# Weight blocks requested from a buffer that was read a step earlier, and a new order at the end of the second transform step

## The chip, the cores and the metric

The kernel runs on one core of one Trainium2 chip. The metric is the device time of one execution in microseconds (us). The engines are TensorE (PE; its weight loads are PEld), VectorE (DVE), ScalarE (ACT), GpSimd (POOL) and SyncE (SP). Each runs its own instructions in the order of the program and waits on semaphores for the others. SyncE and ScalarE also issue transfers (SPq, ACTq); an instruction that issues one waits, like any other, until what it needs is free, and what stands behind it on its engine waits too.

## The reference

```python
h_mlp  = np.maximum(pos_emb @ w1, 0.0) @ w2           # (S, 64) -> (S, 128), S = 12480
h_filt = h_mlp * np.exp(-0.01 * np.arange(S))[:, None]
y = irfft(rfft(x * v, 2 * S) * rfft(h_filt, 2 * S), 2 * S)[:S]   # along the sequence
x = x * y                                             # (S, 128)
h = x @ moe_w_in                                      # (S, 2048)
x = (h * np.clip(h + 3.0, 0.0, 6.0) / 6.0) @ moe_w_out
h = x @ moe2_w_in
out = np.where(h > 0, h, np.exp(np.minimum(h, 0.0)) - 1.0) @ moe2_w_out
```

The result is float32. The four weight matrices of the two feed-forward layers come as float64.

## The kernel before, in words

The long convolution is done as a transform in steps, all of them matmuls with tables.

**First step.** Products `x * v` and the hidden filter layer go through a table of cosines and sines of length 98 into `Au` (two halves of 64 channels each: half 0 lies in `qb`, half 1 in `au`) and `Rk`.

**Second step.** The 91 frequencies are taken in twelve `OCTETS` of eight (the last, number 11, has three). For an octet `o`: `second_r` (L370) transforms the filter's hidden part in place with a table `gm`, ScalarE copies it back (L371); `second_h` (L379) multiplies by `w2`, ScalarE copies the result into a buffer `hss[o % 2]` (L382, two copies) and adds a negated third part (L383); `second_u(o, hf)` (L389) transforms the signal of half `hf` with `gm` into a PSUM bank; `second(o, hf, z)` is the complex product: two VectorE multiplications (L403) into one of two pairs of buffers, then one GpSimd addition (L408) that writes `Au` back. Written h9, r10, z(9,0) and so on below. `gm` comes in groups of four frequencies, eight of them in SBUF; `load_gm0` (L248) on SyncE requests a group two octets ahead. PSUM has four buffers of two banks, tags `px` and `py` with two each. Octets 0 to 9 go one after the other, both halves of each. For octets 10 and 11, half 0 of both comes first, then half 1 of both, with each product cut into pieces of four frequencies.

**Third step.** `third` (L416) takes four channels at a time: eight matmuls into a bank pair `q`, a ScalarE copy of one part into `tb` (L420), and two VectorE operations (L422) that write `Q` over `qb`. 16 groups for half 0, 18 for half 1 (the last three have two, one and one channel). Behind every eight channels of half 1 a piece of `xT` (728 KB) is requested on SyncE into the part of `au` that was read.

**Fourth step.** `fourth` (L496) makes the output in 33 calls, tables `ti` streaming through five buffers on SyncE (L464), VectorE multiplying by `x` (L541).

**Feed-forward layers.** From 286 us to the end, TensorE alternates L616 and L660; this part is not touched.

**Weight conversion.** Beside all this the float64 weights are turned into float32, in 32 blocks of 128 x 256 (`weight_steps`, a generator). One turn k is: VectorE L208, L209, L210 on block k, a GpSimd addition (L213), `load(k + 3)` (L186) into one of three raw buffers, `begin(k + 1)` (ScalarE L196 and L197), `store(k - 1)` (L191, on ScalarE's queue). `convert(rate)` adds `rate` to a counter and takes a turn whenever it passes one: in each `second` call, each `third` group (not the last four) and each call of the fourth step, with `RATE[0]`, `RATE[1]`, `RATE[2]`. The requests go out on SyncE in the second step and on ScalarE afterwards. What is left is done at the fourth step's end.

Of the kernel before, what the change touches and what calls it, by code (L numbers as in the profile page):

```python
# [18 lines left out]
S, D, FO, FF = 12480, 128, 64, 2048  # L19
# [11 lines left out]
HD = D // 2  # L31
# [65 lines left out]
def tile_kernel(ctx, tc, xc, vc, xT, posT, w1_d, w2_d, moe_w, t1_d, gm_d, cs_d, ti_d, rows_d, column_d, ratio_d, outT):  # L97
# [11 lines left out]
    def bank(name, shape, tag=None):  # L109
        if tag is None:  # L110
            turn[0] += 1
            tag = "px" if turn[0] % 2 else "py"
        return ps.tile(shape, F32, tag=tag, name=name)
# [21 lines left out]
    qb = big.tile([128, 2 * QW], F32, name="qb")  # L135
# [19 lines left out]
    OCT = 8  # L155
# [24 lines left out]
    def weight_steps(jobs, raws, es, rs):  # L180
        v = nc.vector

        def load(k):
            if k < len(jobs):
                i, c = jobs[k]
                queue[0].dma_start(raws[k % 3].bitcast(I64), moe_w[i][:, c:c + WC])  # L186

        def store(k):
            if k >= 0:
                i, c = jobs[k]  # L190
                nc.scalar.dma_start(w_dram[i][:, c:c + WC], rs[k % 4])  # L191

        def begin(k):
            if k < len(jobs):
                w = raws[k % 3].rearrange("p (n t) -> p n t", t=2)
                nc.scalar.activation(es[k % 2], w[:, :, 1], AF.Abs)  # L196
                nc.scalar.mul(rs[k % 4].bitcast(I32), w[:, :, 0].bitcast(U32), 2.0 ** -29)  # L197

        for k in range(3):
            load(k)  # L200
        yield
        begin(0)
        yield
        for k in range(len(jobs)):
            w = raws[k % 3].rearrange("p (n t) -> p n t", t=2)
            e = es[k % 2]
            i, r = (z.bitcast(I32) for z in (e, rs[k % 4]))
            v.scalar_tensor_tensor(e, e, LEAST, most.to_broadcast([128, WC]), op0=ALU.max, op1=ALU.min)  # L208
            v.tensor_scalar(i, i, 3, 0x3FFFFFFF, op0=ALU.logical_shift_left, op1=ALU.bitwise_and)  # L209
            v.scalar_tensor_tensor(  # L210
                i, w[:, :, 1].bitcast(I32), -0x40000000, i, op0=ALU.bitwise_and, op1=ALU.bitwise_or
            )
            nc.gpsimd.tensor_tensor(out=r, in0=i, in1=r, op=ALU.add)  # L213
            load(k + 3)
            begin(k + 1)
            store(k - 1)
            yield
        store(len(jobs) - 1)

    def cut(buf, size, n):  # L220
        return [buf[:, i * size:(i + 1) * size] for i in range(n)]

    weights = weight_steps(JOBS, cut(cv, 2 * WC, 3), cut(cv[:, 6 * WC:], WC, 2), cut(cv[:, 8 * WC:], WC, 4))
    RATE = (0.67, 0.28, 0.42)
    due = [0.0]

    def convert(n):
        due[0] += n
        while due[0] >= 1:
            due[0] -= 1  # L230
            next(weights, None)
# [13 lines left out]
    def load_gm0(n):  # L245
        if n < len(KGROUPS):
            k0, nk = KGROUPS[n]
            nc.sync.dma_start(gms[n % len(gms)][:, :nk], gm_d[:, k0:k0 + nk])  # L248
# [5 lines left out]
    def groups(sizes):  # L254
        return list(zip(np.cumsum([0] + sizes[:-1]).tolist(), sizes))

    KGROUPS = groups([KC] * (NK // KC) + [NK % KC])
    OCTETS = groups([OCT] * (NK // OCT) + [NK % OCT])
# [80 lines left out]
    for kind, n in order:  # L339
# [13 lines left out]
    bctx = ctx.enter_context(ExitStack())  # L353
    bp = bctx.enter_context(tc.tile_pool(name="bp", bufs=1)).tile([128, HW + 2 * MW], F32, name="bp")
    hss = [z.rearrange("p (k r d) -> p k r d", r=3, d=D) for z in (rest[:, HB:HB + HW], bp[:, :HW])]
    mms = [
        [z.rearrange("p (d k r) -> p d k r", r=2, k=OCT) for z in zs]
        for zs in (
            (rest[:, MB:MB + MW], rest[:, RF + D:RF + D + MW]), (bp[:, HW:HW + MW], bp[:, HW + MW:]),
        )  # L360
    ]

    def gm_of(k):
        return gms[k // KC % GN][:, k % KC]

    def second_r(o):
        k0, nk = OCTETS[o]
        r = bank("r", [128, OCT, N2], "px")
        for j in range(nk):
            nc.tensor.matmul(r[:, j], lhsT=Rk[:, k0 + j], rhs=gm_of(k0 + j), start=True, stop=True)  # L370
        nc.scalar.copy(Rk[:, k0:k0 + nk], r[:, :nk])  # L371

    def second_h(o):
        k0, nk = OCTETS[o]
        hr = [bank("h", [128, OCT, D], "px") for r in range(2)]
        for j in range(nk):
            for r in range(2):
                p = slice(r * FO, (r + 1) * FO)
                nc.tensor.matmul(hr[r][:, j], lhsT=Rk[p, k0 + j], rhs=w2s[p], start=True, stop=True)  # L379
        hs = hss[o % 2]  # L380
        for r in range(2):
            nc.scalar.copy(hs[:, :nk, r], hr[r][:, :nk])  # L382
        nc.scalar.mul(hs[:, :nk, 2], hs[:, :nk, 1], -1.0)  # L383

    def second_u(o, hf, tag="py"):
        k0, nk = OCTETS[o]
        z = bank("z", [128, OCT, D], tag)
        for j in range(nk):
            nc.tensor.matmul(z[:, j], lhsT=gm_of(k0 + j), rhs=Au[hf][:, :, k0 + j], start=True, stop=True)  # L389
        return z  # L390
# [3 lines left out]
    def second(o, hf, z, size=OCT, rate=0):  # L394
        k0, nk = OCTETS[o]
        for a in range(0, nk, size):
            n = min(size, nk - a)
            m1, m2 = (m[products[0] % 2][:, :, :n] for m in mms)
            products[0] += 1
            h = hss[o % 2][:, a:a + n, :, hf * HD:(hf + 1) * HD]  # L400
            flat = h[:, :, 0].unsqueeze(3).to_broadcast([128, n, HD, 2])
            for mm, h in ((m1, flat), (m2, h[:, :, 1:].rearrange("p k r d -> p k d r"))):
                nc.vector.tensor_tensor(  # L403
                    out=mm.rearrange("p d k r -> p k d r"),
                    in0=z[:, a:a + n].rearrange("p k (d r) -> p k d r", r=2), in1=h, op=ALU.mult,
                )
            convert(rate)
            nc.gpsimd.tensor_tensor(  # L408
                out=Au[hf][:, :, k0 + a:k0 + a + n], in0=m1, in1=m2[:, :, :, ::-1], op=ALU.add
            )  # L410

    def third(hf, s0, nd):
        q = bank("q", [128, 2, 4, N2])
        for j in range(nd):
            for r in range(2):
                nc.tensor.matmul(  # L416
                    q[:NK, r, j], lhsT=Au[hf][:, s0 + j, :, r], rhs=cs[:, r * N2:(r + 1) * N2], start=True, stop=True
                )
        qs = tile_of(stb, "tb", [NK, 4, N2], 3)
        nc.scalar.copy(qs[:, :nd], q[:NK, 1, :nd])  # L420
        for o, op in enumerate((ALU.add, ALU.subtract)):
            nc.vector.tensor_tensor(  # L422
                out=Q[:NK, hf, o * HN:(o + 1) * HN, s0:s0 + nd].rearrange("p g d t -> p d g t"),
                in0=q[:NK, 0, :nd].rearrange("p d (g t) -> p d g t", t=2),
                in1=qs[:, :nd].rearrange("p d (g t) -> p d g t", t=2), op=op,
            )

    last = len(OCTETS) - 1
    second_r(0)
    second_r(1)  # L430
    for o in range(last - 1):
        if o == 0:
            z = second_u(o, 0)
            second_h(o)
        else:
            second_h(o)
            z = second_u(o, 0)
        second(o, 0, z, rate=RATE[0])
        if o:
            second_r(o + 1)  # L440
        if o == last - 2:
            second_r(last)
        second(o, 1, second_u(o, 1), rate=RATE[0])
        for n in range(2 * (o > 0)):
            load_gm0(2 * (o - 1) + GN + n)
    zs = {}
    for o in (last - 1, last):
        second_h(o)
        zs[o] = second_u(o, 0)
    for hf in range(2):  # L450
        for o in (last - 1, last):
            second(o, hf, second_u(o, 1, "px") if hf else zs[o], OCT // 2)
    bctx.close()
    stb = sctx.enter_context(tc.tile_pool(name="stb", bufs=3, side="right"))
    lds = cctx.enter_context(tc.tile_pool(name="ldi", bufs=1, reuse_waits="tile"))
# [4 lines left out]
    def load_ti(m0):  # L460
        if m0 < NM:
            n = min(2, NM - m0)
            ti = tile_of(lds, "ti", [NK, 2, 2, H1], TB)
            nc.sync.dma_start(ti[:, :n].rearrange("p j r a -> p j (r a)"), ti_d[:, m0:m0 + n])  # L464
            tis[m0] = ti
# [6 lines left out]
    a, b = xload.pop()  # L472
    nc.sync.dma_start(xp[:, a:b], xT[:, a:b])
    for s0, nd in groups([4] * 16):
        third(0, s0, nd)
        convert(RATE[1])
    for s0, nd in groups([4] * 15 + [2, 1, 1]):
        third(1, s0, nd)
        if (s0 + nd) % EX == 0:
            a, b = xload.pop(0)  # L480
            nc.sync.dma_start(xp[:, a:b], xT[:, a:b])
        if s0 and s0 % 12 == 0 and s0 // 12 < TB:
            load_ti(s0 // 6)
        convert(RATE[1] if s0 < 56 else 0)

# [44 lines left out]
    for m0 in range(0, NM, 2):  # L530
# [9 lines left out]
        o = START.get((m0, 1), 0)  # L540
# [5 lines left out]
        if m0 == 14:  # L546
            nc.vector.tensor_tensor(out=x0[:, 1], in0=xp[:, :TT], in1=x0[:, 0].bitcast(F32), op=ALU.subtract)
        convert(RATE[2])
    convert(1000)
# [189 lines left out]
```

## Time and profile before

| | |
|---|---|
| median of 3 runs | 1362.53 us (1362.12 to 1362.95) |
| the profiled execution | 1363.29 us, of which the span is 1361.5 us |
| busy share of the span | PE 99%, PEld 84%, DVE 84%, ACT 73%, POOL 29% |
| granted TensorE clock, mean | 0.998 of full speed |
| second step ends, third begins (first L416) | 172.99 us |
| fourth step begins (first L496) | 239.05 us |
| feed-forward layers begin (first L616) | 285.80 us |

Times in the rows are microseconds from the start of the span. A releaser is inferred from semaphore events; a wait for several is put down to the one that came last. A busy TensorE is not one at its peak, since matmuls are pipelined, so idle time is the safer reading.

### The profile page before, as it was taken

How to read it: one execution, taken by the hardware profiler on the slowest of the kernel's cores; microseconds unless marked ns; L12 is line 12 of the kernel's file. 1: busy time of each engine (PE TensorE's matmuls, PEld its weight loads, DVE VectorE, ACT ScalarE, POOL GpSimd, SP SyncE). 2: the span in 40 equal slices, each digit the busy share in tenths (PEclk: the TensorE clock that was granted, in tenths of full speed). 3: DMA queues.
4: the chain of work that ended last, by engine and by line, in shares of the span. 5: the costliest groups of instructions: out<-in, count | busy, mean ns of one | idle time of the engine just before them, and what ended most of it. 6: DMA issues, size and time to landing. Idle time of an engine off the chain costs nothing.

```text
span 1361.5 us, 20839 instructions
## 1 busy us (share of the span) xinstructions
PE 1341.5 (99%) x8154; PEld 1149.4 (84%) x8154; DVE 1145.8 (84%) x1230; ACT 991.5 (73%) x1171; POOL 396.2 (29%) x280
## 2 busy tenths in 40 slices
PE   9999988999999999999999999999999999999998
PEld 9999887987888888888888888888888888888898
DVE  6748677689988888888888888888888888888897
ACT  5666523268888778877888778877888778877876
POOL 1027620124322233222322232222322232222223
PEclk9999999999999999999999999999999999999999
DMA  8924316650000000000000000000000000000000
GB/s 271 258 66 133 92 53 229 205 191 1 1 8 9 8 8 1 9 8 8 1 8 8 9 9 1 8 8 8 1 8 8 8 8 1 9 8 8 8 4 16
DMA packets 32491, 58.15 MB, mean 43 GB/s; under 512 B 3880, under 2 KB 12169, under 8 KB 32393
## 3 DMA queue, kind: packets, MB, share of 16 engines
q1 hardware_dynamic: 25048, 47.85, 11.3%
q10 hardware_dynamic: 7344, 8.98, 2.1%
q8 instruction: 64, 1.05, 0.3%
q14 instruction: 35, 0.28, 0.1%
HBM read 46.23 MB, written 10.58 MB: 42 GB/s over the span
## 4 chain that ended last, share of the span: by engine, by line
PE 76%; DVE 4%; issue 2%; ACT 1%; DMA 0%; POOL 0%; ACTq 0%; DVEq 0%; POOLq 0%
PE h L616 37%; PE o L660 37%; PE y L496 3%; DVE gs L650 2%; DVE qb L422 1%; DVE g L637 1%; DMA ti<-in_ti 0%; POOL a L629 0%; ACT tb L420 0%; DVE g L639 0%; ACT a L628 0%; ACT gs L645 0%; DVE cv L208 0%; ACT cv L196 0%; DVE cv L210 0%
## 5 line engine op out<-in xcount | busy, mean ns | idle before, releaser
L660 PE MATMUL o<-gs,w 128*128 128x512 f32 (+1 forms) x2400 | 567.1, 384 | 0.5 <-DVE gs L650 0.4
L660 PEld LDWEIGHTS o<-gs,w 128*128 128x128 f32 x2400 | 445.3, 188 | 88.6 <-DVE gs L650 0.9
L629 POOL TENSOR_SCALAR a<-a 128x1024 f32<-128x1024 f32 (+1 forms) x200 | 296.3, 1481 | 718.3 <-ACT a L628 718.3
L650 DVE TENSOR_TENSOR gs<-g,gs 128x1024 fp32r<-128x1024 f32 (+1 forms) x400 | 483.1, 1208 | 4.5 <-ACT gs L645 3.7
L645 ACT CAST gs<-g 128x1024 fp32r<-128x1024 f32 (+1 forms) x400 | 410.3, 1026 | 54.7 <-DVE g L637 53.1
L637 DVE SCALAR_TENSOR_TENSOR g<-a,h 128x1024 f32<-128x1024 f32 (+1 forms) x200 | 238.7, 1194 | 120.5 <-ACT a L626 120.2
L616 PE MATMUL h<-xs,w 128*128 128x512 f32 (+1 forms) x1200 | 302.0, 387 | 0.6 <-DVE g L637 0.4
L616 PE MATMUL h<-x,w 128*128 128x512 f32 (+1 forms) x1200 | 299.0, 385 | 0.3 <-ACT a L628 0.3
L628 ACT ACTIVATE a<-h 128x1024 f32<-128x1024 f32 (+1 forms) x200 | 201.3, 1007 | 91.6 <-PE h L616 90.5
L616 PEld LDWEIGHTS h<-xs,w 128*128 128x128 f32 x1200 | 223.6, 188 | 48.8 <-DVE g L637 1.6
L616 PEld LDWEIGHTS h<-x,w 128*128 128x128 f32 x1200 | 223.1, 188 | 43.8 <-issue 0.5
L626 ACT ACTIVATE a<-h,bounds 128x1024 f32<-128x1024 f32 (+1 forms) x200 | 219.2, 1096 | 52.1 <-PE h L616 51.7
L639 DVE SCALAR_TENSOR_TENSOR g<-a,h 128x1024 f32<-128x1024 f32 (+1 forms) x200 | 237.5, 1187 | 0.2 <-POOL a L629 0.2
L196 ACT ACTIVATE cv<-cv 128x256 f32<-128x256 f32 x32 | 14.1, 441 | 67.2 <-DVE cv L210 27.0
L213 POOL TENSOR_TENSOR cv<-cv 128x256 int32<-128x256 int32 x32 | 23.4, 730 | 111.1 <-DVE cv L210 111.1
L422 DVE TENSOR_TENSOR qb<-q,tb 91x512 f32<-91x512 f32 (+2 forms) x68 | 39.3, 648 | 16.4 <-ACT tb L420 16.4
L408 POOL TENSOR_TENSOR qb<-qb,bp 128x1024 f32<-128x1024 f32 (+2 forms) x13 | 27.4, 2110 | 71.0 <-DMA qb<-in_gm 70.5
L496 PE MATMUL y<-ti,qb 91*64 91x98 f32 (+1 forms) x1024 | 45.9, 247 | 1.2 <-DMA ti<-in_ti 0.7
L496 PEld LDWEIGHTS y<-ti,qb 91*64 91x64 f32 x1024 | 45.4, 138 | 1.7 <-issue 1.2
L322 PE MATMUL pa<-t,cv 98*64 98x182 f32 x512 | 44.7, 318 | 0.0
L322 PEld LDWEIGHTS pa<-t,cv 98*64 98x64 f32 x512 | 37.7, 137 | 4.0
L416 PE MATMUL q<-cs,au 128*91 128x128 f32 x256 | 29.4, 274 | 5.8 <-DVE qb L422 5.8
(65 smaller groups left out, 803.5 us busy)
## 6 DMA issues: line engine op xcount, KB each, us to landing
uv<-in_xc SPq DMA_DIRECT2D x32, 196.0 KB
out_T<-y SPq DMA_DIRECT2D x23, 256.0 KB
au<-in_xT SPq DMA_DIRECT2D x8, 728.0 KB
qb<-in_gm SPq DMA_DIRECT2D x22, 256.0 KB
cv<-in_mw ACTq DMA_DIRECT2D x18, 256.0 KB
ti<-in_ti SPq DMA_DIRECT2D x32, 139.3 KB
uv<-in_vc SPq DMA_DIRECT2D x22, 196.0 KB
w_scratch<-cv ACTq DMA_DIRECT2D x32, 128.0 KB
```

The source lines that it names most:

```text
L322: nc.tensor.matmul(pa[f * HN:(f + 1) * HN, j, :2 * NK], lhsT=src(j, f), rhs=table[:, f], start=True, stop=True)
L422: nc.vector.tensor_tensor(out=Q[:NK, hf, o * HN:(o + 1) * HN, s0:s0 + nd].rearrange("p g d t -> p d g t"), in0=q[:NK, 0, :nd].rearrange("p ...
L496: nc.tensor.matmul(y[h * HD:(h + 1) * HD, off:off + w], lhsT=Q[:NK, h, j // 2, :, j % 2], rhs=ti[:, m - m0, r, H1 - w:], start=r == 0, sto ...
L616: nc.tensor.matmul(h[:, j], lhsT=wslice(2 * m - 2, a, 2 * u + j), rhs=x[:, b], start=i == 0, stop=i == 2)
L626: nc.scalar.activation(a, h, AF.Relu, bias=three)
L628: nc.scalar.activation(a, h, AF.Exp)
L629: nc.gpsimd.tensor_scalar(a, a, 1.0, 0.0, op0=ALU.min, op1=ALU.max)
L637: nc.vector.scalar_tensor_tensor(g, a, 6.0, h, op0=ALU.min, op1=ALU.mult)
L639: nc.vector.scalar_tensor_tensor(g, a, -1.0, h, op0=ALU.add, op1=ALU.max)
L645: nc.scalar.copy(t[:, 0], g)
L650: nc.vector.tensor_tensor(out=t[:, 1], in0=g, in1=t[:, 0].bitcast(F32), op=ALU.subtract)
L660: nc.tensor.matmul(o[:, :WID[t]], lhsT=wslice(2 * m - 1, a, 2 * u + j), rhs=gs[:, b, j], start=u == 0 and j == 0 and i == 0, stop=u == NU ...
```

## The change

The first two weight blocks, instead of three, are requested at the start, and turn k requests block k + 2, whose raw buffer was read in turn k - 1. The rates become 0.78, 0.3 and 0.45. The third step takes no turn in its first eight groups. In the second step octets 0 to 8 go as before; then come octets 9, 10, 11 with half 0 of all three (products in pieces of four, and for octet 9 a rate of 0.5 a piece), with r10 and r11 behind octet 9's product, and then half 1 of all three with whole products. Octet 11 gets a filter buffer of its own, `Rs`, over the part of `qb` that octets 0 and 1 used.

```diff
-        for k in range(3):
+        for k in range(2):
             load(k)
...
-            load(k + 3)
+            load(k + 2)
             begin(k + 1)
             store(k - 1)
...
-    RATE = (0.67, 0.28, 0.42)
+    RATE = (0.78, 0.3, 0.45)
...
+    Rs = qb[:, :3 * D * OCTETS[-1][1]].rearrange("p (k r d) -> p k r d", r=3, d=D)
...
+    last = len(OCTETS) - 1
+
+    def hs_of(o):
+        return Rs if o == last else hss[o % 2]
...
-        hs = hss[o % 2]
+        hs = hs_of(o)
...
-            h = hss[o % 2][:, a:a + n, :, hf * HD:(hf + 1) * HD]
+            h = hs_of(o)[:, a:a + n, :, hf * HD:(hf + 1) * HD]
...
-    for o in range(last - 1):
+    for o in range(last - 2):
...
-        if o == last - 2:
-            second_r(last)
         second(o, 1, second_u(o, 1), rate=RATE[0])
         for n in range(2 * (o > 0)):
             load_gm0(2 * (o - 1) + GN + n)
-    zs = {}
-    for o in (last - 1, last):
+    ends = range(last - 2, last + 1)
+    for o in ends:
         second_h(o)
-        zs[o] = second_u(o, 0)
-    for hf in range(2):
-        for o in (last - 1, last):
-            second(o, hf, second_u(o, 1, "px") if hf else zs[o], OCT // 2)
+        second(o, 0, second_u(o, 0), OCT // 2, rate=0.5 if o == last - 2 else 0)
+        if o == last - 2:
+            second_r(o + 1)
+            second_r(last)
+    for o in ends:
+        second(o, 1, second_u(o, 1, "py" if o == last - 1 else "px"))
...
-        convert(RATE[1])
+        convert(RATE[1] if s0 >= HD // 2 else 0)
```

## Rows read from the trace of the kernel before

**Rows 1.** Chain that ended last, in order of time: start us, us, what.

```profile
199.31 3.94 issue
...
257.20 6.14 DMA ti<-in_ti
```

**Rows 2.** Windows: stretch, its length, busy us of PE, PEld, DVE, ACT, POOL, PEclk, DMA share, GB/s.

```profile
172.99:239.05 66.06, 58.06 (x512) 56.19 (x513) 48.88 (x92) 22.37 (x49) 9.36 (x11) 1.00 0.45 145
203.35:239.05 35.70, 29.39 (x258) 28.08 (x257) 26.28 (x49) 13.54 (x30) 3.61 (x5) 1.00 0.66 218
239.05:285.62 46.57, 45.88 (x1024) 45.37 (x1024) 32.81 (x78) 11.85 (x29) 11.62 (x15) 1.00 0.71 213
```

**Rows 3.** Waits in the third step: us in total, times, longest us.

```profile
PE q L416 <- DVE qb L422: 7.5, 8, 1.7
```

**Rows 4.** Timeline of one conversion, third step: start, us, engine, line, idle before it.

```profile
187.66 0.41 DVE L208 SCALAR_TENSOR_TENSOR cv<-cv,bounds 128x256 f32<-128x256 f32 x1
...
188.43 0.43 DVE L210 SCALAR_TENSOR_TENSOR cv<-cv 128x256 int32<-128x256 int32 x1
188.94 0.34 ACTq L186 DMA_DIRECT2D cv<-in_mw  x1
...
189.38 0.43 ACT L196 ACTIVATE cv<-cv 128x256 f32<-128x256 f32 x1 [4.39 <-DVE cv L210]
...
190.05 1.53 ACT L420 COPY tb<-q 91x512 f32<-91x512 f32 x3
190.65 4.87 DVE L422 TENSOR_TENSOR qb<-q,tb 91x512 f32<-91x512 f32 x8 [1.79 <-ACT tb L420]
...
192.08 7.20 PE L416 MATMUL q<-cs,qb 128*91 128x128 f32 x64 [1.13 <-DVE qb L422]
```

**Rows 5.** Timeline from octet 8 to the third step's start.

```profile
142.06 2.06 PE L379 MATMUL h<-qb 64*128 64x128 f32 x32
...
149.36 0.43 DVE L210 SCALAR_TENSOR_TENSOR cv<-cv 128x256 int32<-128x256 int32 x1
149.69 2.06 PE L379 MATMUL h<-qb 64*128 64x128 f32 x32
149.87 1.23 DVE L403 TENSOR_TENSOR qb<-z,qb 128x1024 f32<-128x1024 f32 x1
...
153.65 0.42 DVE L210 SCALAR_TENSOR_TENSOR cv<-cv 128x256 int32<-128x256 int32 x1
...
154.57 0.38 SPq L248 DMA_DIRECT2D qb<-in_gm  x1
...
157.22 2.37 POOL L408 TENSOR_TENSOR qb<-qb,bp 128x1024 f32<-128x1024 f32 x1
...
158.03 0.93 PE L370 MATMUL r<-qb 128*128 128x128 f32 x6 [2.48 <-DMA qb<-in_gm]
...
159.00 0.48 ACT L371 COPY qb<-r 128x384 f32<-128x384 f32 x1 [2.39 <-PE r L370]
...
164.37 1.93 ACT L382 COPY qb<-h 128x1024 f32<-128x1024 f32 x2 [4.24 <-PE h L379]
...
166.33 1.06 ACT L383 ACTIVATE qb<-qb 128x1024 f32<-128x1024 f32 x1
...
169.13 1.28 POOL L408 TENSOR_TENSOR qb<-qb,bp 128x512 f32<-128x512 f32 x1
169.21 0.69 DVE L403 TENSOR_TENSOR qb<-z,qb 128x512 f32<-128x512 f32 x1 [1.09 <-POOL au L408]
...
172.99 13.26 PE L416 MATMUL q<-cs,qb 128*91 128x128 f32 x117 [2.31 <-POOL qb L408]
...
176.96 1.06 ACT L420 COPY tb<-q 91x512 f32<-91x512 f32 x2 [8.27 <-POOL au L408]
```

**Rows 6.** Windows: the granted clock (PEclk) behind the hole, columns as in rows 2.

```profile
160.00:162.00 2.00, 2.00 (x12) 2.00 (x10) 0.00 (x0) 0.13 (x1) 0.00 (x0) 0.50 0.19 61
```

**Rows 7.** Line L208 in 98 to 173: count, ns min/median/max, first and last start.

```profile
L208 DVE SCALAR_TENSOR_TENSOR cv<-cv,bounds x11: 411/435/1128, 102.8 to 164.8; 128x256 f32<-128x256 f32 x11
```

More of the change, by code (lines that the diff above doesn't have):

```diff
@@ L426, in third @@
             )
-    last = len(OCTETS) - 1
     second_r(0)
     second_r(1)
-    for o in range(last - 1):
+    for o in range(last - 2):
         if o == 0:
```

## The prediction

> **What bounds the kernel now.** I read the chain of waits first. Its traced part begins in the third step, and there the longest piece is no work: ScalarE waits 3.94 us before it may issue a weight load [rows 1]. The windows by stage say what that is worth: in 172.99 to 239.05 TensorE is busy for 58.06 of 66.06 us, so 8.0 us are lost, 6.3 of them in the second half; the fourth step is full (45.88 of 46.57) [rows 2]. The list of waits puts 7.5 of the 8.0 on VectorE's `L422` [rows 3]. The timeline of one conversion tells why [rows 4]: `load(k+3)` writes the raw buffer that `L210` of the same step still reads, so ScalarE, in order, stands until `L210` ends (188.43+0.43), issues the load at 188.94, does its two conversion operations, and only then copies the three groups that TensorE has meanwhile finished. VectorE, idle for 1.79, starts at 190.65, and TensorE, with no free bank, resumes at 192.08.
>
> The second step is TensorE's (7.63 us from one octet's `L379` to the next, 142.06 to 149.69, so 3.81 a call of `second`), until its end. There `L370` waits 2.48 us for the last `gm` group: SyncE could issue that load only at 154.57, behind a weight load that waited for the `L210` at 153.65; it landed 3.5 us later [rows 5]. After this hole the granted clock is 0.50, the 1.2 GHz level, in 160 to 162 [rows 6]. The third step begins at 172.99 when GpSimd has finished the first channels' sums, and its first copy waits until 176.96 for GpSimd's last sum of all [rows 5].
>
> **The weight request.** `load(k+2)` goes into the buffer that step k-1 read, free for a whole step. ScalarE then passes it at once. With a conversion every 1/0.30 = 3.33 groups, and 58.06/32 = 1.81 us of TensorE a group, the period is 6.05 us. ScalarE needs in it 3.33 x 0.51 + 0.34 + 2 x 0.43 and a store, some 3.2; VectorE 3.33 x 1.22 + 1.2 = 5.3 [rows 4]. Both are under 6.05, four banks lie between, so TensorE sets the pace. Of the 8.0 us about 0.5 at the hand-over to the fourth step stays: I take 7.4 off. Bounds: 8.0, and half of it, 3.7, if VectorE's 1.2 us block still empties the banks.
>
> The added wait: `begin(k+1)` needs a block that is now requested one step before it instead of two. Behind it on ScalarE stand the copies of `q`, and VectorE waits for those. The trace shows no landing of such a block by itself; the nearest rows are 3.5 us for 192 KB [rows 5] and 6.14 us for a `ti` pair in the fourth step [rows 1]. Three groups give 5.4 us. So a conversion costs between nothing and 0.7, over the four in the second half 0 to 2.8; I take 0, since half a microsecond of ScalarE is covered by the banks. In the second step the requests are SyncE's and only let `gm` loads pass earlier.
>
> **The rates.** The counts: 18 x 0.78 + 2 x 0.5 = 15 turns before the third step (13 now), 22 x 0.30 = 6.6 in it (8 of 30 x 0.28 now), so 13 conversions are left for the fourth step as now. Two conversions move under the second step's TensorE. VectorE's cost there is not the third step's: `L208` takes 0.41 to 1.13 us [rows 7], and two conversions in successive calls end 4.28 us apart (149.36, 153.65) against 3.81 of TensorE [rows 5]. At 0.78 there are runs of three and four such calls (2-4, 6-9, 11-13, 15-18); after four VectorE is some 1.3 us late. A `z` bank is wanted again only 7.63 - 1.9 = 5.7 us after it is filled and VectorE reads it for 2 x 1.23, so 3 us of lateness are hidden: nothing, at most 1 us.
> In the third step, where GpSimd is busy for 9.4 of 66 us [rows 2], `L208` takes 0.41 [rows 4]; in the second, under `L408`, up to 0.7 more. The Trainium skill (SBUF — State Buffer, "Who interferes with whom") says that a VectorE instruction with two SBUF inputs and a GpSimd instruction that reads SBUF exclude each other for a whole instruction. By the rows the fourth call ends 1.3 us late; by the rule alone it could stand for a full `L408` (2.37) and end some 1.6 later still, which would leave 1.2 of the 2.8 us below. No row here shows a wait of that length.
>
> **The second step's end.** In the new order (a group of 16 matmul pairs takes 7.63/4 = 1.9):
> - h9 and z(9,0) stay at 149.7 to 153.5. r10 and r11 (three columns) follow until 156; the `gm` group is no longer late (its load passes at about 151).
> - ScalarE must copy r10 and r11 before h10. It stands ahead of that in `begin`, which waits for GpSimd's half of the conversion in call 18: the fourth in its run, `L210` at about 155.0, GpSimd to 155.85. Then 0.86 + 1.0 + 0.48 [rows 4, 5]: h10 at 158.2. So TensorE's hole is not gone: 156 to 158.2, 2.2 us, now behind ScalarE.
> - h10 takes 2.0, ScalarE's copies 1.93 and the negation 1.06: 163.2. VectorE's half product 0.69, then GpSimd 1.28 for each half of octet 10 and about 1.0 for octet 11: 167.5. The third step's matmuls can start at about 168.
> - (9,1): its buffer is free at 166.5; VectorE 2.45 to 169, GpSimd 2.37 to 171.3; (10,1) to 173.7; (11,1), three columns, to 174.8. Unsplit products leave GpSimd idle for 1.5 here, which is in the sum.
> - The first copy at 174.85, 0.51 and 1.22 later the first bank comes free: the fifth group starts at 176.6. Now it starts at 172.99 + 4 x 1.81 = 180.2. Gain 3.6.
> Whether the clock falls is open: the hole of 2.48 us was followed by 0.50, one of 2.31 (before 172.99) by 1.00 [rows 2, 5, 6]. At 1.2 GHz h10 and z(10,0) take 1.8 us more, which passes straight down this chain: gain 1.8. As no row separates the two, I take 2.8; bounds 0.5 (clock low and VectorE later) and 4.5 (the lateness after four calls absent).
>
> **The fourth step** has 0.7 us of idle [rows 2], with a `ti` pair that took 6.14 us [rows 1] against five calls of 45.88/33 = 1.39 each: little room. The transfers' engines are busy for 0.66 of the half before it [rows 2]; the same bytes in 29 instead of 35.7 us make 0.8, and `xT`'s last piece will land deeper in the fourth step. Cost 0.5, between 0 and 4. Conversions end two calls earlier; the tail of this step waits for TensorE's last matmuls anyway: nothing. What follows is rigidly shifted.
>
> **Sum.** 7.4 + 2.8 - 0.5 = 9.7 off the profiled execution's 1363.29 (span 1361.5 and 1.8 around): 1353.6. That execution lies 0.76 above the median of the runs shown, so 1352.8 for a median; I say 1353.0.
>
> **Rivals.**
> - Half of the third step's stall stays, VectorE's block being the cause rather than ScalarE's wait: 1352.8 + 3.7 = 1356.5. For it: VectorE would be busy 5.3 of 6.05. Against: in rows 4 VectorE is idle just when TensorE is.
> - The hole only moves: the end of the second step gives 0.5 or less, 1355 to 1356. For it: ScalarE's order behind `begin`; against: half the products are off the path to the third step.
> - Transfers crowd: the second half's `xT` and weights take 29 us of nearly full engines, `ti` comes late, 3 to 4 us are given back: 1356 to 1357.
> - Slower than before: blocks come too late in the fourth step. There a conversion has 1.39/0.45 = 3.1 us; two blocks are in flight, so with a landing of T one takes (T+1.3)/2 (1.3: ScalarE's issues and its two operations). Over 13 of them it must lose 9.7 + 2.7 us, 0.95 each: T above 6.8 us on the mean, each further us 6.5 us. The longest landing in the rows is 6.14, and that is one of many; then 1365 or more.
> - The change's requests still wait (the buffer's reader isn't done): the third step stays, 1360.
>
> **Numbers.** The forecast 0.62 (its own range 1350 to 1355.5); half stall 0.1; hole moves 0.1; crowding 0.1; late blocks 0.04; no effect 0.04. About 0.2% (2.7 us) is what a measurement tells from no change. The first four are faster: 0.92; same 0.04; slower 0.04. The range takes in the upper rivals and the bounds 8.0 + 4.5: 1349.8 to 1357.2.
>
> **What would show it.** In the third step, `L196` no longer waits for `L210`, and TensorE's idle is under 1.5 us. `L370` has no wait on `gm`; a wait of `L379` on ScalarE's `L371` of about 2 us stands at 156 to 158. The first `L420` comes 1 to 3 us after 173. TensorE starts `L496` at 228 to 230 instead of 239.05 and needs 46 to 48 us for it. Wrong if `L496` begins after 233, if the fourth step takes over 49, or if `L196` waits for `in_mw`.

## The result and the profile after

The changed kernel takes 1350.93 us (median of 4 runs, 1349.69 to 1352.01) against 1362.55 for the kernel before (median of 4, 1362.12 to 1362.95): ratio 0.9914, interval 0.9897 to 0.9932. Forecast were 1353.0 and 1349.8 to 1357.2: faster, as said, and by 2 us more. Beside the times compared here, 14 of the 36 executions of the kernel before took 1403 to 1406 us at a mean granted clock of 0.965 to 0.968, and none of the nine of the changed kernel did; they are left out of every ratio.

The profiled execution of the changed kernel is its fastest: 1349.69 us, span 1347.9, mean clock 1.000. Line numbers are shifted by 5 or 6: `L496` is now `L501`, `L420` `L426`, `L379` `L385`; the weight lines keep theirs.

| stage (start to start, us) | before | after | gain |
|---|---|---|---|
| up to h9 | 149.69 | 149.56 | 0.1 |
| h9 to the third step | 23.30 | 19.09 | 4.2 |
| third step | 66.06 | 58.10 | 8.0 |
| fourth step | 46.75 | 45.82 | 0.9 |
| feed-forward layers | 1075.70 | 1075.33 | 0.4 |

The windows of the changed kernel, columns as in [rows 2]: third step, its second half, fourth step.

```profile
168.65:226.75 58.10, 56.27 (x514) 55.89 (x513) 48.76 (x86) 22.65 (x45) 10.09 (x9) 1.00 0.45 145
198.31:226.75 28.44, 28.10 (x258) 27.92 (x257) 25.42 (x49) 12.71 (x26) 3.65 (x5) 1.00 0.80 260
226.75:272.50 45.75, 45.52 (x1024) 45.32 (x1024) 32.63 (x78) 12.06 (x29) 12.29 (x16) 1.00 0.78 233
```

TensorE's idle time in the third step fell from 8.0 us to 1.8, and in the second half from 6.3 to 0.3, though the transfers' engines are now busy for 0.80 of that half instead of 0.66. The waits (us in total, times, longest), third step, then fourth:

```profile
ACT tb L426 <- POOL au L414: 10.2, 1, 10.2
PE q L422 <- DVE qb L428: 1.5, 1, 1.5
...
ACT cv L196 <- DMA cv<-in_mw: 18.1, 7, 5.6
```

The eight waits of [rows 3] are one now, of 1.5 us, at the fifth group. A conversion in the third step of the changed kernel, to be laid beside [rows 4]:

```profile
198.31 28.11 PE L422 MATMUL q<-cs,au 128*91 128x128 f32 x256
...
209.03 0.58 ACT L426 COPY tb<-q 91x512 f32<-91x512 f32 x1 [1.17 <-PE q L422]
209.04 0.34 ACTq L186 DMA_DIRECT2D cv<-in_mw  x1
...
209.51 0.44 ACT L196 ACTIVATE cv<-cv 128x256 f32<-128x256 f32 x1
...
210.78 0.58 ACT L426 COPY tb<-q 91x512 f32<-91x512 f32 x1 [0.49 <-PE q L422]
210.85 0.41 DVE L208 SCALAR_TENSOR_TENSOR cv<-cv,bounds 128x256 f32<-128x256 f32 x1
...
211.62 0.42 DVE L210 SCALAR_TENSOR_TENSOR cv<-cv 128x256 int32<-128x256 int32 x1
```

The request (`L186`) stands 2.6 us ahead of the `L210` of its turn instead of behind it, ScalarE goes straight on, and one row of TensorE, without a break, covers all 16 groups of the second half: 28.11 us, 1.757 a group. The end of the second step, beside [rows 5]:

```profile
147.56 2.38 POOL L414 TENSOR_TENSOR au<-qb,bp 128x1024 f32<-128x1024 f32 x1
148.94 1.28 DVE L208 SCALAR_TENSOR_TENSOR cv<-cv,bounds 128x256 f32<-128x256 f32 x1
...
151.50 0.38 SPq L248 DMA_DIRECT2D qb<-in_gm  x1
...
153.66 2.72 PE L376 MATMUL r<-qb 128*128 128x128 f32 x22
154.87 0.42 DVE L210 SCALAR_TENSOR_TENSOR cv<-cv 128x256 int32<-128x256 int32 x1
155.78 0.73 POOL L213 TENSOR_TENSOR cv<-cv 128x256 int32<-128x256 int32 x1 [1.55 <-ACT bp L389]
...
156.55 0.43 ACT L196 ACTIVATE cv<-cv 128x256 f32<-128x256 f32 x1 [0.94 <-POOL cv L213]
157.20 1.38 ACT L377 COPY qb<-r 128x1024 f32<-128x1024 f32 x2
158.26 2.43 PE L385 MATMUL h<-qb 64*128 64x128 f32 x32 [1.88 <-ACT qb L377]
...
168.65 7.15 PE L422 MATMUL q<-cs,qb 128*91 128x128 f32 x64
...
175.25 1.07 ACT L426 COPY tb<-q 91x512 f32<-91x512 f32 x2 [10.22 <-POOL au L414]
...
177.29 21.17 PE L422 MATMUL q<-cs,qb 128*91 128x128 f32 x192 [1.50 <-DVE qb L428]
```

`L376` runs its 22 columns without a wait. The hole has moved: h10 waits 1.88 us for ScalarE, which stands behind `L196`, GpSimd's `L213` and the fourth conversion of a run. The clock held here (1.00 in 160 to 162, against 0.50 in [rows 6]). By their mean clock it doesn't always: the executions have one of 1.000 (1349.69, 1350.13) or 0.998 to 0.999 (1352.01, 1351.74).

### The profile page after: what moved, and what is told of

Same layout as the page of the kernel before. It is cut to its first block, busy times and chain, and to the rows that moved or that the text cites. A ratio compares the mean times of both kernels' runs of the same rounds, so it can differ in the third digit from the quotient of the medians.

```text
span 1347.9 us, 20844 instructions
## 1 busy us (share of the span) xinstructions
PE 1337.7 (99%) x8154; PEld 1148.6 (85%) x8154; DVE 1149.0 (85%) x1230; ACT 993.0 (74%) x1171; POOL 395.4 (29%) x280
## 4 chain that ended last, share of the span: by engine, by line
PE 87%; DVE 5%; issue 2%; POOL 2%; ACT 2%; DMA 1%; SPq 0%; POOLq 0%; DVEq 0%; ACTq 0%
PE h L621 37%; PE o L665 37%; PE pa L322 4%; PE q L422 4%; PE y L501 3%; DVE gs L655 1%; PE z L395 1%; DVE bp L409 1%; DVE qb L409 1%; DMA uv<-in_vc 1%; PE h L385 1%; DVE g L642 1%; DVE cv L208 1%; PE r L376 1%; POOL qb L414 1%
## 5 line engine op out<-in xcount | busy, mean ns | idle before, releaser
L621 PEld LDWEIGHTS h<-xs,w 128*128 128x128 f32 x1200 | 223.6, 188 | 48.5 <-DVE g L642 1.4
L213 POOL TENSOR_TENSOR cv<-cv 128x256 int32<-128x256 int32 x32 | 23.3, 729 | 97.5 <-DVE cv L210 96.0
L414 POOL TENSOR_TENSOR qb<-qb,bp 128x1024 f32<-128x1024 f32 (+2 forms) x14 | 27.6, 1975 | 71.6 <-DMA qb<-in_gm 70.4
L426 ACT COPY tb<-q 91x512 f32<-91x512 f32 (+2 forms) x34 | 18.7, 557 | 39.1 <-PE q L422 27.2
L501 PE MATMUL y<-ti,qb 91*64 91x98 f32 (+1 forms) x1024 | 45.7, 247 | 0.6 <-issue 0.3
L501 PEld LDWEIGHTS y<-ti,qb 91*64 91x64 f32 x1024 | 45.3, 138 | 0.9 <-ACT tb L426 0.5
L322 PEld LDWEIGHTS pa<-t,cv 98*64 98x64 f32 x512 | 40.7, 137 | 3.4 <-POOL cv L268 0.5
L196 ACT ACTIVATE cv<-cv 128x256 f32<-128x256 f32 x32 | 14.2, 444 | 38.8 <-POOL cv L213 19.4
```

Source lines behind the costliest of these rows:

```text
L322: nc.tensor.matmul(pa[f * HN:(f + 1) * HN, j, :2 * NK], lhsT=src(j, f), rhs=table[:, f], start=True, stop=True)
L501: nc.tensor.matmul(y[h * HD:(h + 1) * HD, off:off + w], lhsT=Q[:NK, h, j // 2, :, j % 2], rhs=ti[:, m - m0, r, H1 - w:], start=r == 0, sto ...
L621: nc.tensor.matmul(h[:, j], lhsT=wslice(2 * m - 2, a, 2 * u + j), rhs=x[:, b], start=i == 0, stop=i == 2)
```

## The experiments

All ratios are against the kernel before on the same chip. The changed kernel, measured twice, has means 0.3 us apart, so less than 1 us between two versions is not resolved.

**The changed kernel once more** (x_changed_again), as the measure for x_request_only, x_no_request and x_old_rates, which ran on the same chip.

> The changed kernel again, for its spread and its granted clocks. Theory: its executions fall into two groups some 1.8 us apart, about 1350 with a mean granted clock of 1.000 and about 1352 with 0.998 or 0.999, according to whether the clock falls behind the 1.9 us wait of L385 on L377. Rival: the spread is noise that the clock does not go with; then the clocks and the times are unordered.

Measured: 1351.12 us (1349.86 to 1352.4), 0.9915 [0.9899, 0.9930]. With the first measurement there are nine executions: five at a clock of 1.000 have a mean of 1350.27, four at 0.998 to 0.999 one of 1352.11. The difference is 1.84; the prediction had worked out 1.8 for a clock that falls behind the hole.

**The request alone** (x_request_only): the kernel before with two lines changed.

```diff
-        for k in range(3):
+        for k in range(2):
...
-            load(k + 3)
+            load(k + 2)
```

> The kernel before with range(2) and load(k + 2) alone; old rates, old order. Theory: the request carries nearly all of the gain: the third step's 8.0 us of idle fall to about 1 (-7), the last gm group is requested at about 150 instead of 154.6, so the 2.5 us wait of L370 and the slow clock behind it go (-4): 1351 to 1352. Rival (the new order of the last octets is what shortens the second step's end): 1354 to 1356, with the third step still starting at 172 or later.

Measured: 1349.68 us (1349.34 to 1350.81), 0.9907 [0.9890, 0.9924]: the whole gain, by two lines, and 1.3 us more than its theory gave. Its timeline:

```profile
149.75 0.38 SPq L248 DMA_DIRECT2D qb<-in_gm  x1
...
153.09 2.62 PE L370 MATMUL r<-qb 128*128 128x128 f32 x22
...
157.47 2.06 PE L379 MATMUL h<-qb 64*128 64x128 f32 x32
...
168.18 29.86 PE L416 MATMUL q<-cs,qb 128*91 128x128 f32 x256 [2.31 <-POOL qb L408]
...
197.87 28.11 PE L416 MATMUL q<-cs,au 128*91 128x128 f32 x256
```

The window of its third step, columns as in [rows 2]:

```profile
168.18:226.32 58.14, 57.80 (x513) 57.62 (x513) 49.45 (x92) 24.11 (x49) 9.34 (x11) 0.97 0.54 164
```

The load of the last `gm` group passes at 149.75 instead of 154.57, `L370` doesn't wait, and in the old order there is no hole ahead of h10. The fall of the clock comes here behind the 2.31 us ahead of the third step; TensorE is at half speed (0.50 in 168.6 to 172) while VectorE and GpSimd still finish the second step, and the second half begins at 197.87, no later than in the changed kernel (198.31); counted from h9, both take the same to there (48.70 and 48.75 us).

**All but the request** (x_no_request): the changed kernel with `range(3)` and `load(k + 3)` back.

> The changed kernel with range(3) and load(k + 3) put back; new rates, new order. Theory: six conversions in the third step each cost TensorE about 0.9 us again (+5), and the last gm group is late behind L210 once more (+3): 1357 to 1360. Rival (the new rates, with no conversion in the first eight groups, are what emptied the stall): below 1354.

Measured: 1405.04 us (1403.66 to 1406.32, six executions), 1.0309 [1.0294, 1.0325]. All expectations missed it. The timeline, from SyncE's requests to the fourth step:

```profile
151.43 4.62 SPq L186 DMA_DIRECT2D cv<-in_mw  x2
...
156.15 0.38 SPq L248 DMA_DIRECT2D qb<-in_gm  x1
...
160.11 1.62 PE L376 MATMUL r<-qb 128*128 128x128 f32 x6 [4.05 <-DMA qb<-in_gm]
...
238.27 2.33 PE L422 MATMUL q<-cs,au 128*91 128x128 f32 x8 [2.10 <-DVE qb L428]
...
240.62 87.39 PE L501 MATMUL y<-ti,qb 91*64 91x97 f32 x1024
```

Windows in the fourth step and in the feed-forward layers behind it:

```profile
240.00:320.00 80.00, 79.98 (x935) 79.66 (x935) 32.33 (x76) 11.14 (x28) 11.18 (x15) 0.50 0.44 124
340.00:360.00 20.00, 19.84 (x85) 15.43 (x84) 20.00 (x20) 18.26 (x22) 1.29 (x1) 1.00 0.04 14
```

The old request in the new order lets the `gm` load pass at 156.15 (the weight load ahead of it waits for a conversion), and the third step has its stalls back. Behind the last of them, 2.10 us, the granted clock falls to 0.50, and the fourth step takes 87.3 us (to 327.94) instead of 45.8 with TensorE busy all the time. At a held clock the span would be about 240.62 + 45.82 + 1075.33 = 1361.77, some 1363.6 with the 1.8 around it: no faster than before. Nor is it faster where the clocks are alike: the six executions of the kernel before on this chip with a mean clock of 0.965 to 0.968 took 1403.48 to 1405.62 us.

**The new order alone** (x_order_only): as x_no_request, and the rates too as before.

```diff
-    RATE = (0.78, 0.3, 0.45)
+    RATE = (0.67, 0.28, 0.42)
...
-        convert(RATE[1] if s0 >= HD // 2 else 0)
+        convert(RATE[1])
```

> The new order of the last octets alone, with load(k + 3), range(3), the old rates and conversions from the third step's first group. Theory (the order is worth nothing by itself): the last gm group is late behind L210 as before, L376 waits 2.5 us or more for it, and the third step keeps some 8 us of idle: 1360 to 1364 where the granted clock holds; where it falls in the third step's second half, as in the kernel without the request, the fourth step takes 87 instead of 46 us and the time is 1402 to 1406. Rival (the order shortens the second step's end by about 3 us by itself): 1357 to 1359.5.

Measured: 1406.45 us (1405.27 to 1407.76, six), 1.0322 [1.0309, 1.0335], with the clock at 0.50 for 88.75 us from 241.0 on. The timeline has both waits still:

```profile
158.32 0.91 PE L376 MATMUL r<-qb 128*128 128x128 f32 x6 [2.87 <-DMA qb<-in_gm]
...
238.74 0.65 PE L422 MATMUL q<-cs,au 128*91 128x128 f32 x4 [2.95 <-DVE qb L428]
239.89 60.41 PE L501 MATMUL y<-ti,qb 91*64 91x97 f32 x708 [0.50 <-issue]
```

The third step begins 1.9 earlier than before (171.09), but its first copy still waits for GpSimd's last sum (until 177.68), so its fifth group starts only 0.3 earlier (179.73). The fourth step begins 0.8 later than before (239.89 against 239.05): at a held clock the order alone is worth nothing. Why TensorE's clock falls in every execution of these two kernels, and in some of the kernel before, was not settled.

**Request and order, old rates** (x_old_rates): the changed kernel with the diff just shown.

> The changed kernel with the old rates 0.67, 0.28, 0.42 and conversions from the third step's first group (octet 9's pieces keep 0.5). Theory: the rates are worth little: 1350 to 1352.5, third step idle under 2.5 us. Rival (the rates carry the third step's gain): 1354 or more.

Measured: 1349.98 us (1348.82 to 1351.38), 0.9906 [0.9890, 0.9921], every clock 1.000. The same places of the timeline:

```profile
157.05 2.42 PE L385 MATMUL h<-qb 64*128 64x128 f32 x32 [0.49 <-ACT qb L377]
...
176.07 21.17 PE L422 MATMUL q<-cs,qb 128*91 128x128 f32 x192 [1.49 <-DVE qb L428]
...
265.04 7.31 PE L501 MATMUL y<-ti,qb 91*64 91x98 f32 x168 [1.13 <-DMA ti<-in_ti]
```

The hole is 0.49 instead of 1.88 and the fifth group comes 1.2 earlier: the run of four conversions that the rate 0.78 makes is what holds ScalarE. In this profile the fourth step gives the 1.2 us back: with the wait for `ti` and one of 0.77 behind it, it takes 47.57 us (225.54 to 273.11) instead of 45.82. The medians on this chip differ by 1.1 us, but the changed kernel's five executions at a clock of 1.000 have a mean of 1350.27 and these five one of 1350.01. So what the new rates cost here is in the main the clock that falls behind the hole, in four of nine executions; a cost beside that is not resolved.

**Request and new rates, old order** (x_request_rates): x_request_only with `RATE = (0.78, 0.3, 0.45)`.

> The kernel before with range(2), load(k + 2) and the new rates, old order of the octets. Theory: the old order with the request ends at 1350.0, and the new rates cost about 1 us only where a conversion stands ahead of the copies of r10 and r11; here octet 9's first call has no such run, so 1349.3 to 1351. Rival (the new order is needed with the new rates): 1352 or more.

Measured: 1351.39 us (1349.76 to 1352.48, six), 0.9916 [0.9898, 0.9934], clocks 0.997 to 0.999. That lies between the two expectations. It was measured on another chip than x_request_only, so the times alone don't show that the rates cost something in the old order too. Its timeline, beside that of x_request_only:

```profile
169.64 29.81 PE L416 MATMUL q<-cs,qb 128*91 128x128 f32 x256 [2.87 <-POOL qb L408]
```

From h9 to the third step it takes 19.92 us (149.72 to 169.64), x_request_only 19.01 (149.17 to 168.18): 0.9 more.

**The copies ahead of the conversion** (x_copies_first): the changed kernel with r10 and r11 issued before octet 9's product.

```diff
         second_h(o)
-        second(o, 0, second_u(o, 0), OCT // 2, rate=0.5 if o == last - 2 else 0)
+        z = second_u(o, 0)
         if o == last - 2:
             second_r(o + 1)
             second_r(last)
+        second(o, 0, z, OCT // 2, rate=0.5 if o == last - 2 else 0)
```

> The changed kernel with r10 and r11 issued ahead of octet 9's product, so that ScalarE copies them before it waits for GpSimd's half of the conversion. Theory: the 1.9 us wait of L385 on L377 shrinks to about 0.5, the second step's end is 1.2 us shorter, and no execution has the slow clock there: 1348.7 to 1350, all clocks 1.000. Rival (the new rates cost their 1 us elsewhere, in VectorE's lateness): 1350.5 to 1351.5.

Measured: 1350.09, 1349.51, 1350.2 and 1348.66 (mean 1349.6, clock 1.000), and one execution, the profiled one, of 1372.1; ratio without the latter 0.9903 [0.9890, 0.9917]. The wait ahead of h10 is 0.43, so it was ScalarE's order behind `begin` that made the hole; against the changed kernel at a clock of 1.000 (1350.27) that is 0.7 us, less than is resolved. The long execution shows by itself what the clock costs. Its timeline has a wait in the fourth step:

```profile
157.06 2.43 PE L385 MATMUL h<-qb 64*128 64x128 f32 x32 [0.43 <-ACT qb L377]
...
250.29 4.01 PE L502 MATMUL y<-ti,qb 91*64 91x98 f32 x60 [1.93 <-DMA ti<-in_ti]
```

Windows ahead of this wait, behind it, and in the feed-forward layers (from 294.22):

```profile
240.00:248.00 8.00, 8.00 (x194) 8.00 (x190) 6.33 (x16) 1.78 (x5) 2.19 (x3) 1.00 0.83 237
256.00:290.00 34.00, 34.00 (x423) 34.00 (x421) 12.95 (x29) 4.92 (x11) 8.08 (x9) 0.50 0.42 119
296.00:310.00 14.00, 13.92 (x60) 10.58 (x59) 11.76 (x11) 12.54 (x14) 1.30 (x1) 1.00 0.75 235
```

The wait of 1.93 us is for `ti`; then come the fall at 251.56, and 44.37 us at 0.50. Half of that is 22.2, and the execution is 22.5 longer than the mean of the others.

**A fourth raw buffer** (x_fourth_buffer): from the third step on, free space of `au` holds a fourth block, requested two turns ahead.

```diff
+        def raw(k):
+            return raws[k % 3 if k < 15 else (k - 16) % 4]
...
-            load(k + 2)
+            ask(k + 2 + (k > 12))
...
+    raws.append(au[:, S:S + 2 * WC])
```

> The changed kernel with a fourth raw buffer from the third step on, so that a block is requested two turns ahead and still waits for nobody. Theory (the added wait is covered): L196's waits for in_mw in the fourth step, 18 us in the changed kernel, go, and the time stays within 0.7 us of 1351. Rival (the late blocks cost TensorE something in the fourth step): 1349 or less.

Measured: 1352.27 us (1350.61 to 1353.28), 0.9922 [0.9909, 0.9934]: not faster, and outside the 0.7 us that the theory allowed; four of the five executions have a clock of 0.999. The waits for `in_mw` in the fourth step are gone; ScalarE waits there for GpSimd instead, and the step takes 45.59 us (228.45 to 274.04) against 45.82. So blocks that come late there cost some 0.2 by these two profiles. From the list of waits of its fourth step (lines stand 5 or 6 further on than in the changed kernel):

```profile
ACT cv L202 <- POOL cv L218: 27.3, 11, 4.6
```

The profiled execution also shows the predicted other case, the clock falling behind the same hole. Its timeline there:

```profile
158.49 3.64 PE L391 MATMUL h<-qb 64*128 64x128 f32 x32 [1.88 <-ACT qb L383]
162.06 2.47 PE L401 MATMUL z<-qb 128*128 128x128 f32 x16
```

And the window of [rows 6]:

```profile
160.00:162.00 2.00, 2.00 (x19) 1.83 (x16) 1.43 (x4) 0.25 (x1) 0.64 (x2) 0.50 0.00 0
```

With the same wait of 1.88, h10 takes 3.64 here and 2.43 in the changed kernel's profile, and from h10 to the third step it is 11.97 us (158.49 to 170.46) instead of 10.39 (158.26 to 168.65), 1.6 more.

**Banks that don't wait for GpSimd's last sum** (x_free_tb): old rates, and every third copy of `q`, the first among them, goes to free space of `au`, which needs no room that the second step still uses.

```diff
+    turns = [0]
...
-        qs = tile_of(stb, "tb", [NK, 4, N2], 3)
+        if turns[0] % 3:
+            qs = tile_of(stb, "tb", [NK, 4, N2], 2)
+        else:
+            qs = au[:NK, S:S + 4 * N2].rearrange("p (d g) -> p d g", d=4)
+        turns[0] += 1
...
-    stb = sctx.enter_context(tc.tile_pool(name="stb", bufs=3, side="right"))
+    stb = sctx.enter_context(tc.tile_pool(name="stb", bufs=2, side="right"))
```

> The changed kernel with the old rates, and every third copy of q goes to a place in au that nothing else uses, so that the first copy doesn't wait for GpSimd's last sum. Theory: the third step's fifth group no longer stands for 1.5 us: 1348 to 1349 (old rates alone: 1350.0). Rival (the first bank comes free no sooner, VectorE being still at the products): within 0.5 of 1350.

Measured: 1347.55 us (1346.82 to 1348.2, four), 0.9888 [0.9874, 0.9901], the fastest of all and a little below what was expected. The first copy comes at 169.39 instead of 175.25; the second and third still wait for GpSimd's last sum (174.05), but the bank that the first one frees is enough for TensorE. In the timeline neither half of the third step has an interruption:

```profile
167.45 28.11 PE L424 MATMUL q<-cs,qb 128*91 128x128 f32 x256
...
195.39 28.11 PE L424 MATMUL q<-cs,au 128*91 128x128 f32 x256
...
223.85 40.65 PE L507 MATMUL y<-ti,qb 91*64 91x97 f32 x906 [0.35 <-issue]
```

The fourth step begins 2.9 earlier than in the changed kernel and takes 46.36 us (to 270.21), 0.5 more.

**Both of the last repairs** (x_best): x_free_tb with the copies first.

> The changed kernel with the old rates, the place in au for every third copy of q, and r10 and r11 ahead of octet 9's product. Theory: the last 0.5 us of L385's wait on L377 goes: 1346.8 to 1347.8, every clock 1.000 as far as no ti load is late. Rival (the chain over GpSimd's sums ends at the same time whenever octet 10 starts): 1347.5, as without it.

Measured: 1348.52 us (1347.61 to 1349.36), 0.9895 [0.9877, 0.9913]: outside both expectations and no better than x_free_tb. The wait ahead of h10 was small already with the old rates (0.49, here 0.43), and in its profile the fourth step begins 0.2 earlier (223.63) and takes 48.5 us (to 272.15), with this row in its timeline:

```profile
249.26 17.76 PE L508 MATMUL y<-ti,qb 91*64 91x98 f32 x416 [1.61 <-DMA ti<-in_ti]
```

The clock held behind this wait (1.00 in 250 to 267).

**Fewer tables in flight** (x_four_ti): the changed kernel with `TB = 4` instead of 5, to make a wait for `ti` and see whether the clock falls behind it.

> The changed kernel with four ti buffers instead of five, so that TensorE waits for ti in the fourth step. Theory (a wait of about 2 us there lets the granted clock fall, and through the rest of the fourth step it stays at 1.2 GHz): executions of 1365 to 1400 with mean clocks of 0.97 to 0.99, the earlier the wait, the longer. Rival (the waits cost only their own length): 1352 to 1358 with clocks of 0.999 or 1.000.

Measured: 1354.33 us median of six; five at 1353.99 to 1355.68 (clock 0.999 to 1.000), one, profiled, at 1389.2. The timeline of that one:

```profile
237.59 73.55 PE L501 MATMUL y<-ti,qb 91*64 91x98 f32 x904 [1.49 <-DMA ti<-in_ti]
```

Behind this wait of 1.49 the clock is 0.50 from 237.8 to 312.9; feed-forward matmuls began at 311.07. So a fall can follow a wait in the fourth step and need not: five of six executions came out as the rival has it.

## Why the prediction was right, and where it was off

**The weight request: right in kind, mis-sized.** ScalarE's wait behind `L210` was the cause: the request alone takes the stalls away, and VectorE's own block of 1.2 us costs nothing ([rows 4] against 28.11 us without a break). From the fifth group to the fourth step the two profiles have 59.0 (239.05 less 172.99 + 4 x 1.757 = 180.0) and 49.5 us: 9.6, where 7.4 was said. The term started from idle time, 8.0. But TensorE's busy time of 58.06 counted a tail of some 0.2 us behind each of nine interruptions (four groups take 7.20 in [rows 4] and 4 x 1.757 = 7.03 undisturbed); 32 undisturbed groups take 56.2, so 9.8 were lost, and the pace of 1.81 us was 3% too long.

**The second step's end: right sum, wrong cause.** The hole moved to 158.26 (said: 158.2) behind ScalarE's `L377` (before: `L371`), the third step began at 168.65 (about 168), the first copy at 175.25 (174.85), the fifth group at 177.29 (176.6): 2.7 gained with the clock held, where 3.6 was said for that and 2.8 taken. (The table's 4.2 us at the third step's start are 2.7 at the fifth group, which waits for the first copy and so for GpSimd's last sum. Part of the gain is the clock that was low in the profile of before: z(9,1) takes 3.58 us there behind the hole, and 2.00 in octet 8's place.) That 2.7 lies beside 2.8 is luck: 2.8 stood between the two cases of the clock, and this profile is one of them. So is the hole's end: GpSimd's `L213` ended at 156.51 and not 155.85, but h10 waited for the first of ScalarE's two copies only. What failed is the step that gave this gain to the new order. The request alone gives it in the old order (from h9 to the third step 19.01 us against 19.09), since SyncE's `gm` load no longer stands behind a weight load; the order alone gives nothing. The prediction had seen that `gm` loads pass earlier and didn't work out what the old order would make of it.

**The clock: both cases occur.** It was left open whether it falls behind this hole, at a price of 1.8. By their mean clocks it does in four of nine executions, and the price is 1.84 by the means and 1.6 by the stretch from h10 to the third step in the profile of x_fourth_buffer.

**The rates.** Costed at nothing to 1 us, taken as nothing. The fourth `L210` of the run ended at 155.29 (said: 155.0). The `L208` of the turn before it took 1.28 us and ended at 150.22, 0.28 behind GpSimd's `L414` (149.94). The Trainium skill (SBUF — State Buffer, "Who interferes with whom") says that the one that issues later stands until the other is done; the trace agrees. It came 1.4 us into `L414`, so it lost 0.9 and not a whole 2.37. The cost came through ScalarE instead: 1.4 us of the hole ahead of h10, and the clock's chance to fall.

**The fourth step.** Said: 46.75 and 0.5 more; it took 45.82. `L196` does wait for `in_mw` (18.1 us in seven waits), which the prediction had called a sign of being wrong. It isn't one: with these waits gone the step is 0.2 shorter. The rival of late blocks asked for 0.95 us lost per conversion; ScalarE has slack enough there. Crowding transfers cost TensorE 0.2 (one wait for `ti`).

**The sum.** 9.6 + 2.7 + 0.9 + 0.4 = 13.6 between the profiled executions. The medians differ by 11.6, since the profiled one of before lies 0.74 above its median and half of the four executions after have the low clock. No rival came in: no half stall, no loss in the fourth step, and the requests did not wait. Three signs lie outside what was said: the third step's idle is 1.8 us and not under 1.5 (1.5 of it the fifth group's wait), `L501` starts at 226.75 and not at 228 to 230, and the fourth step takes 45.8 us and not 46 to 48.

## What to carry to other kernels

A request on an engine's queue waits for the last reader of its buffer, and so does everything behind it: ask for a block into the buffer whose reader is a turn old, even if the block comes one turn later. To size a stall, count undisturbed groups of the same work elsewhere in the trace rather than subtract busy time. And test the smallest part of a change first: here two lines were all of it, the new order was worth nothing, and the new rates cost up to a microsecond, in the main through the clock.

## What was not expected of the hardware

Behind waits of 1.5 to 3 us late in the third or inside the fourth step the granted clock could fall to 0.50, the 1.2 GHz level, and stay there to the end of the fourth step although TensorE was then busy for 34.00 of 34.00 us (x_copies_first); it rose only 1.7 to 3.6 us after the feed-forward matmuls began (at 330, 330, 296 and 313 us in the four profiles that show it). Of the executions with the new request two of 50 fell so, both behind a wait for `ti`. Behind the hole in the second step it rose again some 4 us after TensorE went on (6.5 in x_no_request, where the hole was 4.05). The Trainium skill (TensorE: Matmul & The Clock Gate, "What's actually happening") says that activity releases the throttle; in the second step and the feed-forward layers the trace agrees, in the fourth step it does not. Whether it is the fourth step's matmuls (91 rows, 64 columns of weights) that keep the clock down was not tried. The price is large: a wait of 1.93 us cost 22 more, and one at the step's start 41.5 (87.3, from 240.62 to the first feed-forward matmul at 327.94, against 45.8).
